# Last stage of a gated Fourier and Mish layer: unused weight buffers become operand pairs, and y is added to the first half's results by an accumulating transfer

## The chip, the cores and the metric

The kernel runs on one core of one Trainium2 chip. The metric is device time in microseconds (us), the median of three runs. Before the change it is 867.15 us (866.71 to 867.68).

## What is computed

x is 2048 tokens by 640. The reference, cut to what matters:

```
g = sigmoid((x * gate_w).sum(-1))
y = real(DFT_seq(DFT_hidden(x)))            # as products with cosine and sine matrices
h = x @ w1 + b1                             # 640 -> 1728
b = mish(h) @ w2                            # 1728 -> 640
out = g * y + (1 - g) * b
```

All in float32. The kernel holds every product transposed: features in partitions, tokens in columns, in tiles of 128 by 512. The tokens make four column tiles t = 0 to 3.

## The kernel before

**Products.** A float32 operand is split in two halves for TensorE: h is the value rounded by ScalarE's copy to the type float32r (line 316), l is the rest, which VectorE gets by a subtraction (line 317). A product is three matmuls, hh, hl and lh (`mm3`, line 326). Moving operands lie in pairs of 128x512 tiles (pool R, ten pairs, named r0h, r0l and so on), stationary ones in pairs of 128x640 tiles (pool W, 26 pairs, named w0h, w0l and so on). The large products use a two-by-two scheme with seven block products in place of eight (`Stage` for the sums of the stationary side, `Problem` for the moving side), so many operands are sums of loaded tiles, made by VectorE (`tt`, line 287, recorded as line 289).

**Stages.** First the DFT along the sequence (four problems), then the DFT along the features (two problems, `hd`), whose results, already multiplied by g, are stored as y in memory (`ysc`, 20 tiles of 128x512, names y). Then w1 and Mish, stored in memory as act (`asc`); for tiles t = 2 and 3 act is multiplied by 1 - g at once (`out_act`, line 639). Last comes the product with w2, as two problems (`ou`, line 814): the first half for t = 0 and 1, the second for t = 2 and 3. Each has three parts: `first`, `second`, `third`. Both `first` parts run ahead, and the partial sums of the second half's are stored in memory (names po) and loaded again at the head of its `second` (lines 421 to 424).

**How y gets in.** In the second half (`y` given) the y tiles are loaded and added into the sums as the work goes on, since act was scaled before (`add_y`, line 481). In the first half (`y` is None, `q` is 1 - g) each of ten results is multiplied by 1 - g after its last matmul (`done`, line 535, and `give`, line 543), and `plus` (line 548) loads the y tile into a buffer of pool FS and adds it with VectorE; then `put_out` stores the result on SyncE's queue.

**Order and buffers.** The code doesn't issue instructions as it runs. It makes a graph of operations (`Graph.add`), each with an engine and a planned duration, and `Graph.run` (line 121) plans it: an event simulation at build time with one list of ready operations per engine, sorted by the time at which each is wanted. TensorE's order is fixed, one matmul each 0.2267 us; all wants are worked back from it (`wants`, line 84). Work that empties a bank, and what follows such work of ScalarE or VectorE, is `prompt` and is wanted early. An operation takes buffers from pools when it is planned to start; buffers are kept back for whoever wants them earlier (`granted`, line 146). The planned order is then the order of each engine's instructions and of each queue, and an instruction waits, in order, for what it depends on. A transfer is planned as 2.2 us plus its bytes at 370 GB/s, all transfers one after another (`dma`, line 267). Loads are on SyncE's queue (SP, SPq in the profile, line 276), stores of intermediate results on GpSimd's (POOL, line 285), stores of the output on SyncE's.

**Pools.** FS holds 18 tiles of 128x512 (names f), X six of 128x640 (names x). When nobody asks for an x tile any more, freed x tiles pass to FS (`heir`, lines 206 to 208): a name x on a 128x512 operation of the last stage is such a tile. W has no heir. The last stage's weights take three pairs for each of six row blocks, two shared pairs (`T2`) and two for the remaining rows (`w2_rest`).

Of the kernel before, what the change touches and what calls it, by code (L numbers as in the profile page):

```python
# [12 lines left out]
OP = mybir.AluOpType  # L13

S, D, F = 2048, 640, 1728
P = 128
N = 512
# [7 lines left out]
NR, NFS, NX, NW = 10, 18, 6, 26  # L25
# [22 lines left out]
class Graph:  # L48
# [72 lines left out]
    def run(self, pools):  # L121

        self.wants()
        for op in self.ops:
            for v in op.vals:
                if v.pool and (v.ask is None or op.want < v.ask[0]):
                    v.ask = op.want, op.n, id(v)
        for op in self.ops:
            for v in op.vals:
                if v.pool and v.ask[1] == op.n:  # L130
                    also = [u.ask[0] for u in op.vals if u.pool is v.pool and u is not v]
                    if also:
                        v.ask = min(v.ask, (max(also), op.n, id(v)))
        for p in pools:
            p.asks = sorted({v.ask for op in self.ops for v in op.vals if v.pool is p})
            p.soon = sorted({v.ask for op in self.ops if op.prompt for v in op.vals if v.pool is p and v.ask[1] == op.n})
        missing = {op.n: len(op.deps) for op in self.ops}
        free = {e: 0.0 for e in ("PE", "ACT", "DVE", "SP", "POOL")}
        ready = {e: [] for e in free}
        pe = [op.n for op in self.ops if op.engine == "PE"][::-1]  # L140
        for op in self.ops:
            if not missing[op.n]:
                insort(ready[op.engine], (op.want, op.n))
        events, now, left, dma = [], 0.0, len(self.ops), 0.0

        def granted(op, blocked):
            for v in op.vals:
                if v.pool and v.t is None:
                    if v.pool in blocked:
                        return False  # L150
                    p, n = v.pool, bisect_left(v.pool.asks, v.ask)
                    if not op.prompt:
                        n += bisect_left(p.soon, (v.ask[0] + AHEAD,)) - bisect_left(p.soon, v.ask)
                    if len(p.free) <= n:
                        blocked.add(v.pool)
                        return False
            return True

        while left:
            began = False  # L160
            for e, line in ready.items():
                if free[e] > now + 1e-9 or not line:
                    continue
                if e == "PE":
                    i = next((i for i, x in enumerate(line) if x[1] == pe[-1]), None)
                    if i is not None and not granted(self.ops[pe[-1]], set()):
                        i = None
                else:
                    blocked = set()
                    i = next((i for i, x in enumerate(line) if granted(self.ops[x[1]], blocked)), None)  # L170
                if i is None:
                    continue
                op = self.ops[line.pop(i)[1]]
                if e == "PE":
                    pe.pop()
                for v in op.vals:
                    if v.pool and v.t is None:
                        v.pool.asks.remove(v.ask)
                        if v.ask in v.pool.soon:
                            v.pool.soon.remove(v.ask)  # L180
                        v.t = v.pool.free.pop(0)
                op.emit()
                free[e] = now + op.hold
                if e in ("SP", "POOL"):
                    dma = max(now + DELAY, dma) + op.moves
                    end = dma + 0.1
                else:
                    end = now + op.took + 0.03
                heapq.heappush(events, (end, op.n))
                left -= 1  # L190
                began = True
            if began:
                continue
            times = [t for e, t in free.items() if t > now + 1e-9 and ready[e]]
            if events:
                times.append(events[0][0])
            assert times, ("stuck", left, pe and self.ops[pe[-1]].at, [(p.name, len(p.free)) for p in pools])
            now = max(now, min(times))
            while events and events[0][0] <= now + 1e-9:
                op = self.ops[heapq.heappop(events)[1]]  # L200
                for v in op.vals:
                    v.left -= 1
                    if not v.left and v.pool:
                        p = v.pool
                        p.free.append(v.t)
                        if p.heir and not p.asks:
                            p.heir.free += [p.part(t) for t in p.free]
                            p.free = []
                for a in op.after:
                    missing[a.n] -= 1  # L210
                    if not missing[a.n]:
                        insort(ready[a.engine], (a.want, a.n))
# [8 lines left out]
def fnet_mish_gate(ctx: ExitStack, tc: tile.TileContext, xn, xt, c_re, c_im, wd_re, wd_im,  # L221
                   w1a, w1b, b1a, b1b, w2, gw, out):
    nc = tc.nc
# [5 lines left out]
    def pair(name, n):  # L229
        return sb.tile([P, n], F32R, name=f"{name}h"), sb.tile([P, n], F32R, name=f"{name}l")  # L230

    psum = Pool("psum", [pp.tile([P, N], F32, name=f"ps{i}") for i in range(8)])
    R = Pool("r", [pair(f"r{i}", N) for i in range(NR)])
    FS = Pool("f", [sb.tile([P, N], F32, name=f"f{i}") for i in range(NFS)])
    X = Pool("x", [sb.tile([P, D], F32, name=f"x{i}") for i in range(NX)], FS, lambda t: t[:, :N])
    W = Pool("w", [pair(f"w{i}", D) for i in range(NW)])
    b1s = Val(t=sb.tile([P, NF], F32, name="b1s"))
    gcol = Val(t=sb.tile([P, KS], F32, name="gcol"))
    qcol = Val(t=sb.tile([P, KS], F32, name="qcol"))
# [6 lines left out]
    def scratch(name, n, rows=P):  # L246
        return [[dram(f"{name}{i}_{t}", rows) for t in range(TG)] for i in range(n)]

    usc, ysc = scratch("u", 2 * KD), scratch("y", KD)
# [6 lines left out]
    def whole(*vals):  # L256
        return [(v, None) for v in vals]

    def dve(emit, r, w, n=N, more=0.0):
        took = 0.15 + n / 960 + more  # L260
        return G.add("DVE", emit, r, w, took, took - 0.083)
# [5 lines left out]
    def dma(queue, emit, r, w, size):  # L267
        op = G.add(queue, emit, r, w, DELAY + size / RATE, 0.605 if queue == "SP" else 1.0)
        op.moves = size / RATE
        return op  # L270
# [3 lines left out]
    def load(pool, src, of=None, rows=P, cols=N, queue="SP"):  # L274
        v = Val(pool)
        dma(queue, lambda: ISSUE[queue].dma_start(v.t[:rows, :cols], src() if callable(src) else src),  # L276
            whole(of) if of else [], whole(v), rows * cols * 4)
        return v

    def load_of(pool, d, rows=P):  # L280
        return load(pool, lambda: d.t, d, rows)

    def store(d, v, rows=P, queue=None):
        queue = queue or STORES
        dma(queue, lambda: ISSUE[queue].dma_start(d.t, v.t[:rows]), whole(v), whole(d), rows * N * 4)  # L285

    def tt(o, a, b, op, cut=(slice(None),) * 3, rows=slice(None), n=N):
        (x, y, z) = cut
        dve(lambda: nc.vector.tensor_tensor(o.t[rows, x], a.t[rows, y], b.t[rows, z], op=op),  # L289
            whole(a, b), whole(o), n)  # L290
# [50 lines left out]
    class Stage:  # L341
# [17 lines left out]
        def top(self, k):  # L359
            if k in self.XA:  # L360
                return
            w = self.XA[k] = Val(W)
            g = load(X, self.row(k), cols=D)
# [3 lines left out]
        def low(self, k):  # L367
# [10 lines left out]
            if k // KD not in self.T2:  # L378
                self.T2[k // KD] = Val(W)
            b, c = self.XB[k], self.XT13[k] = Val(W), Val(W)  # L380
            split(self.XA[k], 3, t, 2 * P, 2 * P)
# [10 lines left out]
    class Problem:  # L392
# [154 lines left out]

        def plus(self, f, d, t):
            if self.st is fin and not self.y:
                tt(f, f, load_of(FS, ysc[d][t]), OP.add)  # L550
            self.finish(d, t, f)

        def end(self):
# [37 lines left out]
    def w1_block(f):  # L591
        if f in W1:
            return
        ga, gb, t = load(X, w1a[f], cols=D), load(X, w1a[f + FP], cols=D), Val(X)
        a, b, c = W1[f] = Val(W), Val(W), Val(W)
        if f // KD not in T2B:
            T2B[f // KD] = Val(W)
        split(a, 0, ga, 0, D)
# [11 lines left out]
    def w1_rest():  # L610
        if W1C:
            return
        W1C.append(Val(W))
        split(W1C[0], 0, load(X, w1a[FC - 1], cols=D), 0, D)
# [185 lines left out]
    def put_u(m):  # L800
        return lambda d, t, f: store(usc[m * KD + d][t], f)
# [92 lines left out]
```

## Time and profile before

| | us |
|---|---|
| median of three runs | 867.15 |
| profiled execution, device time | 868.05 |
| its span, first to last instruction | 866.3 |
| TensorE (PE) busy | 859.0 |
| VectorE (DVE) busy | 678.2 |
| ScalarE (ACT) busy | 463.1 |
| GpSimd (POOL) busy | 69.4 |

One execution is recorded by the profiler; times in its views count from its first instruction. A row such as `DVE L289 TENSOR_TENSOR f<-f,f` names engine, line of the kernel (that of the helper which records the operation), operation, and output and inputs by tile names, in most views without buffer numbers; ps is a bank of PSUM. What stands in square brackets behind a row is the engine's idle time ahead of it and who ended it. The chain that ended last is followed back from the last instruction to what released each step.

### The profile page before, as it was taken

The numbers are of one execution on the slowest core, as the hardware profiler recorded it, in microseconds if no ns is written. First come the engines' busy times: TensorE is split into PE (matmuls) and PEld (weight loads), VectorE is DVE, ScalarE is ACT, GpSimd is POOL, SyncE is SP. The second block draws the span as 40 slices with busy tenths as digits, with TensorE's granted clock in tenths as the row PEclk, the third lists the DMA queues.
The fourth block names the chain that finished last, engine by engine and source line by source line (L and its number), as shares of the span: only waits on it lengthen the run. The fifth ranks groups of instructions, "written<-read, shape, count | busy, mean of one in ns | idle before, by whom it ended". The sixth has DMA issues, their size and how long they took to land.

```text
span 866.3 us, 11982 instructions
## 1 busy us (share of the span) xinstructions
PE 859.0 (99%) x3772; PEld 709.1 (82%) x3772; DVE 678.2 (78%) x1213; ACT 463.1 (53%) x849; POOL 69.4 (8%) x132
## 2 busy tenths in 40 slices
PE   9999999999999999999999999999999999999998
PEld 7888888888888888888888888888888888887786
DVE  7999997976785577998878999925576997739991
ACT  7765536544553444677553666735655754531541
POOL 0000002001100200002002012111111100000000
PEclk9999999999999999999999999999999999999999
DMA  9986979864956565759854959456363778626943
GB/s 317 345 283 217 361 216 385 282 217 135 362 171 203 171 255 147 258 192 320 311 183 166 341 208 359 158 197 203 126 212 127 269 273 288 188 84 209 369 169 121
DMA packets 103232, 203.50 MB, mean 235 GB/s; under 512 B 12801, under 2 KB 15233, under 8 KB 103169
## 3 DMA queue, kind: packets, MB, share of 16 engines
q1 hardware_dynamic: 92912, 169.57, 58.4%
q0 software_dynamic: 10112, 33.04, 10.3%
q8 instruction: 29, 0.48, 0.2%
q14 instruction: 35, 0.28, 0.1%
q10 hardware_dynamic: 144, 0.13, 0.0%
HBM read 164.40 MB, written 38.29 MB: 234 GB/s over the span
## 4 chain that ended last, share of the span: by engine, by line
PE 96%; DMA 2%; DVE 1%; issue 0%; ACT 0%; SPq 0%; ACTq 0%; DVEq 0%
PE ps L322 96%; DMA out_dram<-f 1%; DVE f L289 1%; DMA f<-act 1%; DMA x<-in_xn_dram 1%; DVE x L289 0%; SPq L276 0%; DVE r7l L317 0%; DVE r9l L317 0%; ACT r1h L316 0%; ACT r7h L316 0%; DVE r3l L317 0%; DVE f L563 0%; ACT f L561 0%; ACT w0h L310 0%
## 5 line engine op out<-in xcount | busy, mean ns | idle before, releaser
L289 DVE TENSOR_TENSOR f<-f,f 128x512 f32<-128x512 f32 x314 | 211.0, 686 | 15.8 <-DMA f<-in_c_im_dram 7.6
L289 DVE TENSOR_TENSOR f<-ps,f 128x512 f32<-128x512 f32 x100 | 65.3, 685 | 42.9 <-PE ps L322 42.7
L298 ACT ACTIVATE f<-ps 128x512 f32<-128x512 f32 x128 | 74.8, 594 | 37.5 <-PE ps L322 29.9
L285 POOL DMA_DIRECT2D u<-f x40 | 21.5, 540 | 321.5 <-DVE f L289 310.3
L316 ACT ACTIVATE r1h<-f 128x512 fp32r<-128x512 f32 x43 | 27.1, 630 | 32.1 <-PE ps L322 15.7
L316 ACT ACTIVATE r2h<-f 128x512 fp32r<-128x512 f32 x41 | 25.9, 631 | 31.1 <-PE ps L322 24.8
L316 ACT ACTIVATE r8h<-f 128x512 fp32r<-128x512 f32 x41 | 25.8, 630 | 28.3 <-PE ps L322 20.9
L586 ACT ACTIVATE f<-f,b1s 128x512 f32<-128x512 f32 x36 | 25.7, 723 | 28.2 <-DVE f L289 28.1
L316 ACT ACTIVATE r9h<-f 128x512 fp32r<-128x512 f32 x39 | 24.5, 629 | 28.0 <-PE ps L322 18.9
L316 ACT ACTIVATE r4h<-f 128x512 fp32r<-128x512 f32 x39 | 24.5, 629 | 27.4 <-PE ps L322 24.2
L285 POOL DMA_DIRECT2D act<-f x52 | 28.2, 542 | 134.6 <-DVE f L289 72.4
L316 ACT ACTIVATE r6h<-f 128x512 fp32r<-128x512 f32 x39 | 24.5, 628 | 25.0 <-PE ps L322 18.7
L316 ACT ACTIVATE r0h<-f 128x512 fp32r<-128x512 f32 x40 | 25.1, 627 | 23.7 <-PE ps L322 18.1
L317 DVE TENSOR_TENSOR r7l<-f,r7h 128x512 fp32r<-128x512 f32 x41 | 28.2, 688 | 12.0 <-ACT r7h L316 11.8
L316 ACT ACTIVATE r5h<-f 128x512 fp32r<-128x512 f32 x41 | 25.7, 628 | 21.9 <-PE ps L322 15.4
L317 DVE TENSOR_TENSOR r2l<-f,r2h 128x512 fp32r<-128x512 f32 x41 | 28.2, 688 | 11.7 <-ACT r2h L316 11.5
L316 ACT ACTIVATE r7h<-f 128x512 fp32r<-128x512 f32 x41 | 25.7, 628 | 21.4 <-PE ps L322 12.5
L317 DVE TENSOR_TENSOR r8l<-f,r8h 128x512 fp32r<-128x512 f32 x41 | 28.2, 688 | 10.3 <-ACT r8h L316 10.2
L317 DVE TENSOR_TENSOR r5l<-f,r5h 128x512 fp32r<-128x512 f32 x41 | 28.2, 688 | 9.8 <-ACT r5h L316 9.7
L317 DVE TENSOR_TENSOR r6l<-f,r6h 128x512 fp32r<-128x512 f32 x39 | 26.8, 688 | 11.2 <-ACT r6h L316 11.0
L317 DVE TENSOR_TENSOR r0l<-f,r0h 128x512 fp32r<-128x512 f32 x40 | 27.5, 688 | 10.2 <-ACT r0h L316 10.0
L317 DVE TENSOR_TENSOR r1l<-f,r1h 128x512 fp32r<-128x512 f32 x43 | 29.6, 688 | 7.2 <-ACT r1h L316 7.1
(1830 smaller groups left out, 2639.0 us busy)
## 6 DMA issues: line engine op xcount, KB each, us to landing
f<-in_c_re_dram SPq DMA_DIRECT2D x128, 256.0 KB, 4.9
f<-in_c_im_dram SPq DMA_DIRECT2D x128, 256.0 KB, 4.4
f<-act SPq DMA_DIRECT2D x86, 256.0 KB, 5.1
f<-u SPq DMA_DIRECT2D x80, 256.0 KB, 4.7
act<-f POOLq DMA_DIRECT2D x52, 256.0 KB, 3.0
f<-in_xt_dram SPq DMA_DIRECT2D x44, 256.0 KB, 5.2
u<-f POOLq DMA_DIRECT2D x40, 256.0 KB, 5.7
x<-in_xn_dram SPq DMA_DIRECT2D x25, 320.0 KB, 5.0
```

The lines of the kernel that those rows point to most:

```text
L285: dma(queue, lambda: ISSUE[queue].dma_start(d.t, v.t[:rows]), whole(v), whole(d), rows * N * 4)
L289: dve(lambda: nc.vector.tensor_tensor(o.t[rows, x], a.t[rows, y], b.t[rows, z], op=op), whole(a, b), whole(o), n)
L298: act(lambda: nc.scalar.activation(o.t, a.t, AF.Copy, scale=scale), whole(a), whole(o))
L316: act(lambda: nc.scalar.activation(r.t[0][:, :N], src.t[:, :N], AF.Copy), whole(src), [(r, 0)])
L317: dve(lambda: nc.vector.tensor_tensor(r.t[1][:, :N], src.t[:, :N], f32(r.t[0][:, :N]), op=OP.subtract), whole(src) + [(r, 0)], [(r, 1)])
L322: G.add("PE", lambda: nc.tensor.matmul(bank.t, w.t[wn][:, k * P:k * P + P], x.t[xn_][:, :N], start, stop, skip_group_check=True), [(w, (k, ...
L586: act(lambda: nc.scalar.activation(o.t[rows], src.t[rows], AF.Mish, **more), whole(src, table) + whole(b1s) * bias, whole(o), more=0.1)
```

## The change

W gets R as its heir: when nobody asks for a weight pair any more, free ones pass to R, cut to 512 columns. The handing on becomes a function, `bequeath`, that is called not only when a buffer is freed but also when one is taken, so that buffers that are free when the last ask is served pass on at once; this holds for X and FS as well.

In the first half of the last stage, `plus` no longer loads y into a buffer and adds it with VectorE. A transfer on GpSimd's queue reads the y tile from memory and adds it to the result tile in SBUF (`accum_op=OP.add`). It is planned as 2.8 times the bytes of a plain transfer. The store to the output, still on SyncE's queue, follows it.

```
+        def bequeath(p):
+            if p.heir and not p.asks:
+                p.heir.free += [p.part(t) for t in p.free]
+                p.free = []
...
                         v.t = v.pool.free.pop(0)
+                        bequeath(v.pool)
...
                         p.free.append(v.t)
-                        if p.heir and not p.asks:
-                            p.heir.free += [p.part(t) for t in p.free]
-                            p.free = []
+                        bequeath(p)
...
-    W = Pool("w", [pair(f"w{i}", D) for i in range(NW)])
+    W = Pool("w", [pair(f"w{i}", D) for i in range(NW)], R, lambda t: (t[0][:, :N], t[1][:, :N]))
...
+    def add_from(v, d):
+
+        dma("POOL", lambda: nc.gpsimd.dma_start(v.t, d.t, accum_op=OP.add), whole(v, d), whole(v), 2.8 * P * N * 4)
...
         def plus(self, f, d, t):
             if self.st is fin and not self.y:
-                tt(f, f, load_of(FS, ysc[d][t]), OP.add)
+                add_from(f, ysc[d][t])
             self.finish(d, t, f)
```

## The prediction

> **What bounds the kernel now.** I read the page's first part, then the chain that ended last, then TensorE's timeline where that chain leaves TensorE, and then, at that place, what the late instructions waited for. The page says that TensorE is busy nearly always:
>
> ```profile
> PE 859.0 (99%) x3772; PEld 709.1 (82%) x3772; DVE 678.2 (78%) x1213; ACT 463.1 (53%) x849; POOL 69.4 (8%) x132
> ```
>
> The chain, in order of time (start, length, what), shows where it isn't:
>
> ```profile
> 6.76 772.58 PE ps L322 x3406
> ...
> 789.57 0.70 DVE f L289
> 790.26 0.02 issue
> 790.28 0.32 SPq L276
> 790.60 0.05 issue
> 790.65 5.96 DMA out_dram<-f
> 796.61 0.02 issue
> 796.63 5.50 DMA f<-act
> ...
> 806.92 55.39 PE ps L322 x243
> 862.32 0.02 issue
> 862.34 0.39 ACT f L561
> ```
>
> For 772.58 us and for the last 55.39 us the chain is nothing but matmuls, 772.58 / 3406 = 0.2268 us apart. The count of matmuls is not touched by the change, nor is the start (6.76 us) or the tail after 862.34. So all that can be gained lies in the 28 us between the two long pieces, where the first half of the last product hands over to the second. TensorE's timeline there (start, length, ...):
>
> ```profile
> 797.07 0.39 PE L322 MATMUL ps<-r5h,w11h 128*128 128x512 f32 x1
> 797.54 0.50 PE L322 MATMUL ps<-r5l,w11h 128*128 128x512 f32 x1
> 797.88 0.40 PE L322 MATMUL ps<-r5h,w11l 128*128 128x512 f32 x1
> 798.98 0.50 PE L322 MATMUL ps<-r5h,w23h 128*128 128x512 f32 x1 [0.70 <-ACT ps L298]
> 799.32 0.39 PE L322 MATMUL ps<-r5l,w23h 128*128 128x512 f32 x1
> ...
> 805.69 0.39 PE L322 MATMUL ps<-r7h,w9l 128*128 128x512 f32 x1
> 806.03 0.50 PE L322 MATMUL ps<-r3h,w20h 128*128 128x512 f32 x1
> 806.92 0.50 PE L322 MATMUL ps<-r3l,w20h 128*128 128x512 f32 x1 [0.39 <-DVE r3l L317]
> 807.26 0.39 PE L322 MATMUL ps<-r3h,w20l 128*128 128x512 f32 x1
> ```
>
> Matmul records overlap, so the idle column (0.70 and 0.39) understates the loss; starts tell it. First stall: 799.32 - 797.07 = 2.25 us for four steps that take 4 x 0.2268 = 0.91, a loss of **1.34 us**. Second: 807.26 - 805.69 = 1.57 us for three steps (0.68), a loss of **0.89 us**. Together **2.23 us**, 0.26% of the run. That is the cap on what this change can win.
>
> Why they are late is read on ScalarE and on SyncE's queue:
>
> ```profile
> 795.61 0.60 ACT L298 ACTIVATE ps<-x 128x512 f32<-128x512 f32 x1 [14.32 <-DMA x<-po]
> ...
> 798.32 0.60 ACT L298 ACTIVATE ps<-f 128x512 f32<-128x512 f32 x1 [0.52 <-DMA f<-po]
> ```
>
> ```profile
> 777.31 0.32 SPq L276 DMA_DIRECT2D f<-y  x1
> ...
> 790.28 0.32 SPq L276 DMA_DIRECT2D x<-po  x1
> ...
> 792.17 1.26 SPq L276 DMA_DIRECT2D f<-po  x1
> ```
>
> First stall: the second half restarts from partial sums kept in memory (po). Their two loads were issued at 790.28 and 792.17, the last copy into a bank began at 798.32 and TensorE went on at 798.98. The chain says why the loads were late: the load at 790.28 had to wait until an add of VectorE (789.57, 0.70 long) had read the buffer that it was to fill. Second stall: a load of act issued at 796.63 waited for a store to release its buffer (790.65 + 5.96), landed after 5.50 us, and went through sums and splits to r3l, for which TensorE waited until 806.92. Both are one shortage: **full-width buffers (18 f and 6 heirs from x)**, of which ten go in turn to y, the first half's addends (a load of y is still issued at 777.31, ahead of the stalled ones). By stretches (length, then busy time and count of TensorE, its weight loads, VectorE, ScalarE and GpSimd, granted clock, share of the DMA engines, GB/s):
>
> ```profile
> 766.00:780.00 14.00, 14.00 (x63) 11.60 (x62) 6.57 (x11) 4.89 (x8) 0.00 (x0) 1.00 0.22 57
> 780.00:795.00 15.00, 15.00 (x68) 12.42 (x67) 15.00 (x27) 0.60 (x1) 0.00 (x0) 1.00 0.45 138
> 795.00:820.00 25.00, 23.82 (x102) 18.55 (x101) 21.91 (x37) 12.86 (x22) 0.00 (x0) 1.00 1.04 384
> ```
>
> Before the handover the DMA engines are at 0.22 of their time and VectorE at 6.57 of 14 us (buffers are full, nobody can run ahead); then VectorE is full for 15 us with results while ScalarE makes almost no operands (0.60 us); then the DMA engines are full at 384 GB/s to catch up.
>
> **The change part by part.** 1. *Ten adds leave VectorE.* The first half gives ten result tiles; each loses an add of this kind:
>
> ```profile
> L289 DVE TENSOR_TENSOR f<-f,f 128x512 f32<-128x512 f32 x8 | 5.4, 684 | 0.0
> ```
>
> ```profile
> 781.76 0.68 DVE L289 TENSOR_TENSOR f<-f,f 128x512 f32<-128x512 f32 x1
> 782.36 0.68 DVE L289 TENSOR_TENSOR f<-ps,f 128x512 f32<-128x512 f32 x1
> ```
>
> Length 0.68, but they start 0.60 apart: 10 x 0.60 = 6.0 us of VectorE, taken out of the stretch around the handover in which VectorE is full (15.00 of 15 us). Elsewhere VectorE has idle time, so the sum counts this only through the stalls: the splits that follow the results can start some 6 us sooner.
>
> 2. *Ten y loads leave SyncE's queue*, and ten buffers that y held up to the adds come free before the handover. The loads next in line (act, po, the second half's y) take them, in the stretch with DMA at 0.22. Ten transfers more there are 10 x 0.26 MB / 384 GB/s = 7 us of the engines against 0.78 x 14 = 11 us idle. That removes the cause of both stalls.
>
> 3. *Four more operand pairs.* Of 26 weight pairs the last stage uses 3 x 6 + 2 + 2 = 22 (three per block row, two shared, two for the remainder), so four pass to R when the last weight buffer is taken. With next to no new operand from 780 to 795, ten pairs lasted to the first stall at 797, 17 us or 1.7 us each; fourteen last 24 us. Before, ScalarE waited for TensorE to free a pair in the stretch before, 720 to 779 (us in total, times, longest):
>
> ```profile
> ACT r8h L316 <- PE ps L322: 5.5, 3, 2.7
> ACT r6h L316 <- PE ps L322: 5.4, 2, 4.6
> ```
>
> That slack makes the four splits ahead free; without it they would cost 4 x 0.6 us of each engine at the handover, which VectorE's 6.0 us cover. The earlier handing on of free x buffers changes at most a few loads by a few us in the same slack: nothing.
>
> 4. *Ten accumulating transfers on GpSimd's queue.* GpSimd issues nothing in any of the stretches shown (x0), so nothing is queued behind an accumulate that waits for VectorE's product. Issue cost, 0.54 us, from the y stores; the nearest rows for landing are the y loads':
>
> ```profile
> L285 POOL DMA_DIRECT2D y<-f x20: 539/539/556, 466.1 to 522.5; - x20
> ...
> DMA to landing us min/median/max: 2.3/4.6/7.8
> ```
>
> ```profile
> f<-y SPq DMA_DIRECT2D x13, 256.0 KB, 4.9
> ```
>
> No accumulate is in the trace. Its share of the DMA engines is no less than a load's 0.68 us (0.26 MB at 384 GB/s); the far end is that the ten go one after another at the median landing of a y load, 4.9 us each, 49 us in all. I take the planner's own coefficient in the diff, 2.8 loads, 1.9 us each, 19 us for the ten; it is nearer the low end, and the engines work on several transfers at once in the trace. Of these 19 us, 7 us are paid back by the loads of step 2. The rest, 12 us, falls on 780 to 820, where the engines were full, but 7 us or more of that stretch's loads are now earlier and TensorE eats only three loads per 21 matmuls (3 x 0.26 MB in 4.8 us, 165 GB/s of 384). Cost to TensorE: **0**; without the cover of operands made ahead, up to the 12 us less the idle time.
>
> The Trainium skill ("Collectives: The Full Stack", "The bandwidth ceiling: the fold count and why AG ≠ RS ≠ AR") says that an add inside a transfer needs two source reads and so runs at about half a copy's rate. By that an accumulate would be two loads, an estimate of 1.4 us each, and the sum would be the same.
>
> 5. *The store waits for the accumulate*, on SyncE's queue, in order: loads are queued behind it and TensorE, later, waits for them. In the planner the store has lost its due time (only vector and scalar work makes its follower prompt), so it goes when no load can. I cost this at 0, hidden by 24 us of pairs.
>
> **Sum.** The profiled execution took 868.05 us (span 866.3 and 1.8 around it), 0.90 over the median of 867.15. 868.05 - 1.34 - 0.89 + 0 = 865.8; against the median 867.15 - 2.23 = **864.9 us**.
>
> **The rivals.** *A. The shortage moves.* The order of all engines in the last 150 us is planned anew; one of the two stalls stays, or a new one of its size comes, since results now hold buffers longer (product, accumulate, store at lowest priority). For: six of the ten result tiles are taken fresh from the same pool, and a transfer of y takes up to 7.8 us to land. Against: a result plus its y were two tiles, now one. It would give 867.15 - 0.89 = 866.3, or up to no gain.
>
> *B. Slower: SyncE's queue stands still.* If the ten accumulates go at the far end, 49 us, where the planner reckons 19, the last lands 30 us after the time at which the planner puts its store into SyncE's queue. Every load behind stands that long. It decides from the point where the delay exceeds the pairs' 24 us: 30 - 24 = 6 us lost in place of the stalls, 864.9 + 6 = about 870. For: stores did hold loads before (5.96 us in the chain), and the engines are full. Against: several transfers overlap, and a queue that stands gives the engines to the accumulates.
>
> Its rule in the Trainium skill ("DMA: Bandwidth & Descriptors", "Issuing engines are not separate DMA queues"): transfers issued on another queue run on the same 16 DMA engines and save issue time only. The trace can't show it for accumulates; it agrees that the engines are what is short at 1.04.
>
> *C. It doesn't do what it says*: the four pairs pass on too late or the planner doesn't use them. Then the y part alone remains, which already frees more buffers than the stalled loads lacked; a result between A and the forecast.
>
> **How the numbers follow.** A measurement of this kernel can tell about 0.2%, 1.7 us, from no change; the forecast's 2.23 lies little above it. Both stalls gone: 0.58, of which 0.06 would measure as no change. A and C: 0.25. B: 0.17. So faster 0.52, within 0.2% 0.31, slower 0.17. The range goes from the cap with the spread of the runs (about 0.5 us) below it, 864.3, to B, 869.9.
>
> **What would show it.** Right: no gap between matmul starts over 0.25 us from 780 to 820; po loaded and copied before TensorE asks; ten y rows on GpSimd at 0.54 us; operands written to w3, w4, w13, w14; DMA well over 57 GB/s from 766 to 780. Wrong: SyncE waiting on f<-y before a store of out, accumulates landing over 10 us after issue, new gaps in TensorE after 800, or a tail after 862.

## The result, and the profile after

| | before | after |
|---|---|---|
| median of 20 runs, us | 867.15 (866.39 to 868.24) | 865.86 (864.72 to 866.23) |
| profiled execution, device time, us | 868.05 | 866.02 |
| its span, us | 866.3 | 864.3 |

The ratio of the times, after to before, is **0.9981, 95% interval 0.9975 to 0.9988**: faster by 1.6 us, between 1.0 and 2.2. (The two medians alone lie 1.29 us apart.) The forecast was 864.9 us, 2.23 us faster (0.9974), just outside this interval.

Line numbers are 4 to 8 higher in the kernel after (L276 is L280, L285 is L289, L289 is L297, L298 is L306, L317 is L325, L322 is L330). The chain that ended last now has one piece of matmuls where it had two with 28 us of other work between them:

```profile
6.97 853.21 PE ps L330 x3762
860.18 0.02 issue
```

853.21 / 3762 = 0.2268 us per matmul over the whole run. TensorE waits nowhere between 780 and 820; by stretches (columns as in the prediction):

```profile
766.00:780.00 14.00, 14.00 (x64) 11.59 (x63) 7.04 (x11) 5.00 (x9) 0.00 (x0) 1.00 0.22 77
780.00:795.00 15.00, 15.00 (x68) 12.43 (x67) 15.00 (x26) 5.74 (x10) 8.91 (x10) 1.00 0.80 157
795.00:820.00 25.00, 25.00 (x112) 20.72 (x111) 11.26 (x18) 5.40 (x9) 0.00 (x0) 1.00 1.07 343
```

From 795 to 820 TensorE was busy 23.82 us and is now busy 25.00. ScalarE makes 5.74 us of operands and copies in the 15 us in which it made almost none. VectorE, full as before from 780 to 795, then has only 11.26 us of work where it had 21.91. The stretch before the handover hardly changed: 0.22 of the DMA engines both times (57 and 77 GB/s).

What took the place of y's loads is seen in SyncE's issues from 745 to 780 (count, size, median us to landing), before and then after:

```profile
f<-y SPq DMA_DIRECT2D x7, 256.0 KB, 2.8
...
f<-act SPq DMA_DIRECT2D x3, 256.0 KB, 2.7
```

```profile
f<-act SPq DMA_DIRECT2D x11, 256.0 KB, 3.0
...
f<-y SPq DMA_DIRECT2D x2, 256.0 KB, 3.5
```

With the buffers named x counted in, eleven loads of y and four of act have become three of y (for the second half) and fourteen of act. Most of them go out before 766.

SyncE's queue and ScalarE show the partial sums (po) of the first stall. All three loads now go out before 756; in the kernel before, two of the three went out at 790 and 792. The copies into the banks end at 787.1:

```profile
745.86 0.54 SPq L280 DMA_DIRECT2D f<-po  x1
...
753.28 0.32 SPq L280 DMA_DIRECT2D f<-po  x1
755.09 0.32 SPq L280 DMA_DIRECT2D x<-po  x1
```

```profile
785.50 0.58 ACT L306 ACTIVATE ps<-x 128x512 f32<-128x512 f32 x1
786.02 0.58 ACT L306 ACTIVATE ps<-f 128x512 f32<-128x512 f32 x1
786.54 0.58 ACT L306 ACTIVATE ps<-x 128x512 f32<-128x512 f32 x1
```

The passed-on pairs are used. The rows of tile w3h from 690 on show it written as an operand in place of a weight (w4h, w13h and w14h have such rows too):

```profile
L324 ACT ACTIVATE w3h<-f x4: 614/634/635, 709.6 to 825.0; 128x512 fp32r<-128x512 f32 x4
```

The ten accumulates (L293) in the rows of tile y (shortest, median and longest in ns), and the packets of the two queues from 780 to 820 (count, MB, share of 16 engines):

```profile
L289 POOL DMA_DIRECT2D y<-f x20: 542/542/556, 466.2 to 523.6; - x20
...
L293 POOL DMA_DIRECT2D f<-y x7: 861/1100/1573, 782.9 to 791.0; - x7
L293 POOL DMA_DIRECT2D x<-y x3: 1030/1362/1923, 787.4 to 789.2; - x3
...
DMA to landing us min/median/max: 2.3/5.7/12.7
```

```profile
q1 hardware_dynamic: 4556, 8.30, 58.8%
q0 software_dynamic: 1440, 2.62, 37.6%
```

An accumulate takes 0.376 x 40 / 10 = 1.5 us of all 16 engines; a plain 0.26 MB takes 0.588 x 40 x 0.262 / 8.30 = 0.74. Stores wait for accumulates on SyncE's queue, 5.8 us at the longest, and TensorE doesn't feel it (times waited in all, how often, longest):

```profile
SPq L289 <- DMA f<-y: 7.8, 3, 5.8
```

### The profile page after: what moved, and what is told of

It is laid out like the page before. It is cut to its first block, busy times and chain, and to the rows that moved or that the text cites. A ratio compares the mean times of both kernels' runs of the same rounds, so it can differ in the third digit from the quotient of the medians.

```text
span 864.3 us, 11968 instructions
## 1 busy us (share of the span) xinstructions
PE 857.2 (99%) x3772; PEld 709.0 (82%) x3772; DVE 672.5 (78%) x1203; ACT 463.5 (54%) x849; POOL 78.7 (9%) x142
## 4 chain that ended last, share of the span: by engine, by line
PE 99%; DMA 1%; SPq 0%; ACT 0%; DVE 0%; issue 0%; ACTq 0%
PE ps L330 99%; DMA x<-in_xn_dram 1%; SPq L280 0%; DVE x L571 0%; ACT x L569 0%; ACT w0h L318 0%; ACTq L569 0%
## 5 line engine op out<-in xcount | busy, mean ns | idle before, releaser
L297 DVE TENSOR_TENSOR f<-f,f 128x512 f32<-128x512 f32 x308 | 206.8, 686 | 17.6 <-DMA f<-in_c_im_dram 6.8
L297 DVE TENSOR_TENSOR f<-ps,f 128x512 f32<-128x512 f32 x99 | 64.8, 684 | 46.1 <-PE ps L330 39.7
L306 ACT ACTIVATE f<-ps 128x512 f32<-128x512 f32 x132 | 77.4, 595 | 37.9 <-PE ps L330 29.9
L289 POOL DMA_DIRECT2D u<-f x40 | 21.6, 543 | 321.6 <-DVE f L297 311.1
L289 POOL DMA_DIRECT2D act<-f x52 | 28.3, 545 | 132.8 <-DVE f L297 71.2
L324 ACT ACTIVATE r2h<-f 128x512 fp32r<-128x512 f32 x38 | 23.9, 630 | 27.2 <-PE ps L330 22.2
L324 ACT ACTIVATE r1h<-f 128x512 fp32r<-128x512 f32 x38 | 23.9, 629 | 24.7 <-PE ps L330 15.5
L324 ACT ACTIVATE r3h<-f 128x512 fp32r<-128x512 f32 x39 | 24.6, 629 | 21.0 <-PE ps L330 14.8
L325 DVE TENSOR_TENSOR r2l<-f,r2h 128x512 fp32r<-128x512 f32 x38 | 26.1, 688 | 10.9 <-ACT r2h L324 10.8
L325 DVE TENSOR_TENSOR r0l<-f,r0h 128x512 fp32r<-128x512 f32 x38 | 26.2, 689 | 10.3 <-ACT r0h L324 10.1
L325 DVE TENSOR_TENSOR r3l<-f,r3h 128x512 fp32r<-128x512 f32 x39 | 26.8, 687 | 9.1 <-ACT r3h L324 9.0
L325 DVE TENSOR_TENSOR r9l<-f,r9h 128x512 fp32r<-128x512 f32 x38 | 26.1, 688 | 9.5 <-ACT r9h L324 9.1
L325 DVE TENSOR_TENSOR r5l<-f,r5h 128x512 fp32r<-128x512 f32 x38 | 26.1, 688 | 9.4 <-ACT r5h L324 9.3
L325 DVE TENSOR_TENSOR r8l<-f,r8h 128x512 fp32r<-128x512 f32 x39 | 26.8, 688 | 8.3 <-ACT r8h L324 8.2
L325 DVE TENSOR_TENSOR r4l<-f,r4h 128x512 fp32r<-128x512 f32 x39 | 26.8, 687 | 7.9 <-ACT r4h L324 7.7
```

The costliest lines, as they stand in the source:

```text
L306: act(lambda: nc.scalar.activation(o.t, a.t, AF.Copy, scale=scale), whole(a), whole(o))
L324: act(lambda: nc.scalar.activation(r.t[0][:, :N], src.t[:, :N], AF.Copy), whole(src), [(r, 0)])
L325: dve(lambda: nc.vector.tensor_tensor(r.t[1][:, :N], src.t[:, :N], f32(r.t[0][:, :N]), op=OP.subtract), whole(src) + [(r, 0)], [(r, 1)])
```

## The experiments

The theory is that both stalls of TensorE came from a shortage of full-width buffers, of which y held ten. The rivals are the four pairs, VectorE's ten adds, and, for the other side, SyncE's queue standing behind accumulates. The last two columns are worked out from all matmul starts of one profile: what the steps between them take over 0.2268 us, summed over a stretch.

| kernel | ratio to before, 95% interval | lost 780 to 812, us | lost 812 to 845, us |
|---|---|---|---|
| before, first profile | | 2.3 | 0 |
| before_again | 1.0003 (0.9995 to 1.0012) | 1.5 | 0 |
| the change | 0.9981 (0.9975 to 0.9988) | 0 | 0 |
| adds_no_loads | 0.9982 (0.9973 to 0.9991) | 0 | 0 |
| loads_no_adds | 0.9993 (0.9984 to 1.0001) | 0.9 | 0 |
| pairs_alone | 1.0000 (0.9992 to 1.0009) | 1.6 | 0 |
| y_alone | 1.0003 (0.9994 to 1.0012) | 0 | 1.7 |
| y_alone_due | 1.0000 (0.9991 to 1.0009) | 0 | 1.7 |
| y_alone_pool | 1.0004 (0.9996 to 1.0013) | 0 | 2.3 |
| y_alone_narrow | 1.0001 (0.9993 to 1.0010) | 0 | 1.7 |
| due | 0.9981 (0.9972 to 0.9989) | 0 | 0 |
| planned_one | 1.0006 (0.9998 to 1.0014) | 0 | 2.2 |
| planned_five | 1.0051 (1.0039 to 1.0063) | 0 | 5.5 |
| added_twice | 1.0055 (1.0043 to 1.0068) | 0 | 6.6 |

**before_again**: the kernel before, no edit.

> The kernel before, unchanged, timed against itself. Every theory expects a ratio of 1.000 within about 0.001. Its second profile shows whether the two stalls of TensorE (1.34 us near 797, 0.89 us near 806 in the first profile) are of a fixed size: if they are, the forecast of 2.23 us stands and the measured 1.3 to 1.7 us has lost something elsewhere; if the second profile has less than 2 us of them, the first was a large sample and the forecast was mis-sized by it.

TensorE's timeline at the same two places:

```profile
796.98 0.39 PE L322 MATMUL ps<-r5h,w11h 128*128 128x512 f32 x1
...
798.45 0.50 PE L322 MATMUL ps<-r5h,w23h 128*128 128x512 f32 x1 [0.29 <-ACT ps L298]
798.78 0.39 PE L322 MATMUL ps<-r5l,w23h 128*128 128x512 f32 x1
...
805.39 0.40 PE L322 MATMUL ps<-r3h,w20h 128*128 128x512 f32 x1
806.08 0.50 PE L322 MATMUL ps<-r3l,w20h 128*128 128x512 f32 x1 [0.29 <-DVE r3l L317]
806.42 0.39 PE L322 MATMUL ps<-r3h,w20l 128*128 128x512 f32 x1
```

The same matmuls wait for the same things, for less: (798.78 - 796.98) - 4 x 0.2268 = 0.89 and (806.42 - 805.39) - 2 x 0.2268 = 0.58, together 1.47 us where the first profile has 2.23. The places are fixed by the plan, the sizes are not.

**adds_no_loads** and **loads_no_adds**: the kernel before with one half of `plus` each.

```
-                tt(f, f, load_of(FS, ysc[d][t]), OP.add)
+                tt(f, f, f, OP.add)
```

> The kernel before, but the ten adds add each result to itself, so no y is loaded for the first half; g y is left out of the first half's output. VectorE has all its work, ten pairs as before, no accumulates; only the ten loads and their buffers are gone. Theory (full-width buffers): both stalls gone, ratio 0.998. Rival (VectorE is full for 15 us at the handover and makes no operands): the second stall stays, 0.9 us, ratio 0.999 to 1.000.

```
-                tt(f, f, load_of(FS, ysc[d][t]), OP.add)
+                tt(f, f, load_of(FS, ysc[d][t]), OP.add, (slice(0, 8),) * 3, n=8)
```

> The kernel before, but each of the ten adds covers 8 of 512 columns; so y is loaded and held as before, while VectorE loses some 0.5 us of each add (the other columns of the first half's output lack g y). The counterpart of the run that had the adds without the loads. Theory (full-width buffers): the partial sums are still loaded late, so the first stall stays, shorter by what VectorE frees sooner, ratio 0.999 to 1.000. Rival (VectorE's adds): both stalls gone, 0.998.

Without the loads both stalls are gone, with ten pairs, no accumulate, and VectorE as full as it can be (third busy time of each row):

```profile
780.00:795.00 15.00, 15.00 (x68) 12.43 (x67) 15.00 (x26) 4.62 (x8) 0.00 (x0) 1.00 0.45 155
795.00:812.00 17.00, 17.00 (x77) 14.08 (x76) 17.00 (x29) 7.67 (x13) 0.00 (x0) 1.00 1.05 367
```

So VectorE being full doesn't by itself make the stalls; leaving out y's loads and their buffers removes them. This run also leaves out the loads' work for the DMA engines.

Without the adds' work, but with the buffers held, 0.9 us are lost, and the time can't be told from no change. The po loads are as late as before (790.8 and 792.8), yet of the first stall only 0.2 us is left, and 0.7 of the second. The expectation had it the other way round: so VectorE's work has a share in how long the first stall lasts. Against this run y_alone, below, also does without the adds and moves the same y with more work of the DMA engines (1.5 us each), but without buffers for it, and has neither stall. So the buffers, not that work, make the difference. No run gives the kernel more buffers, which would be the direct test.

**pairs_alone**: the change, with the old `plus`.

```
-                add_from(f, ysc[d][t])
+                tt(f, f, load_of(FS, ysc[d][t]), OP.add)
```

> The change without the accumulating transfer: four more operand pairs, y loaded and added by VectorE as before. Theory (full-width buffers): operands move out of f buffers into four more pairs, which frees four f buffers of the ten that y holds, so part of the gain: ratio 0.999, one stall stays. Rival (pairs): the whole gain, 0.998. Rival (VectorE's ten adds): no gain, 1.000.

Nothing is gained; 1.6 us are lost as before. The theory's 0.999 was wrong, and this run alone would fit the rival of VectorE's ten adds, which adds_no_loads excludes. SyncE's queue shows that the po loads are as late as they were (790.28 and 792.17):

```profile
790.40 0.32 SPq L280 DMA_DIRECT2D f<-po  x1
...
792.29 0.90 SPq L280 DMA_DIRECT2D x<-po  x1
```

**y_alone**: the change without the heir.

```
-    W = Pool("w", [pair(f"w{i}", D) for i in range(NW)], R, lambda t: (t[0][:, :N], t[1][:, :N]))
+    W = Pool("w", [pair(f"w{i}", D) for i in range(NW)])
```

> The change without the heir of W: y is added by the accumulating transfer, ten operand pairs as before. Theory (full-width buffers were short): both stalls gone or nearly so, ratio 0.998. Rival (the four pairs matter): the ten pairs run out near 797 as before, a stall of 0.5 us or more stays, ratio 0.999 to 1.000.

Neither expectation held. Both stalls at the handover are gone, as the theory has it, yet the time is that of before: new stalls stand 20 us later. TensorE's timeline:

```profile
824.07 0.40 PE L330 MATMUL ps<-r3h,w21h 128*128 128x512 f32 x1
825.23 0.50 PE L330 MATMUL ps<-r3l,w21h 128*128 128x512 f32 x1 [0.77 <-DVE r3l L325]
```

It is not a free pair that lacks. The pair r3 stands empty for over 13 us, from its last matmul to the copy that fills it again, and r1 does so from 807 to 818:

```profile
809.47 0.39 PE L330 MATMUL ps<-r3h,w22l 128*128 128x512 f32 x1
```

```profile
823.15 0.62 ACT L324 ACTIVATE r3h<-f 128x512 fp32r<-128x512 f32 x1
```

So neither part alone brings anything, and the two together bring all of it. (Both parts keep the earlier handing on of free buffers, which no run takes alone.) Three edits of y_alone ask what makes the new stall. **y_alone_due**, in `plus`:

```
                 add_from(f, ysc[d][t])
+                self.finish(d, t, f)
+                G.ops[-1].by = G.pe + 12.0
+                return
             self.finish(d, t, f)
```

> The accumulating transfer without the four pairs, but the ten stores of the first half's results get a due time in the planner, 12 us after the last matmul planned at that place, instead of none. Theory (buffers: results wait for the low-priority store and hold f buffers too long): the stalls near 824 to 833 that the run without the four pairs showed (about 1.5 us) go, ratio 0.998. Rival (the accumulates themselves, their landing of 5 to 13 us and their double share of the DMA engines, hold the buffers): the stalls stay or move, ratio 1.000.

**y_alone_pool**, in `plus`:

```
                 add_from(f, ysc[d][t])
+                return self.finish(d, t, f, "POOL")
             self.finish(d, t, f)
```

> The accumulating transfer without the four pairs, the ten stores issued on GpSimd's queue behind their accumulates instead of SyncE's. SyncE's queue then never stands behind an accumulate (8 us in all, 5.6 at the longest, in the run without the four pairs). Rival B in small (the standing queue makes the stalls near 824): stalls gone, ratio 0.998. Theory (buffers): each result still holds its buffer as long, the next accumulate even waits behind a store, so the stalls stay, ratio 1.000 or more.

**y_alone_narrow**, in `add_from`:

```
-        dma("POOL", lambda: nc.gpsimd.dma_start(v.t, d.t, accum_op=OP.add), whole(v, d), whole(v), 2.8 * P * N * 4)
+        dma("POOL", lambda: nc.gpsimd.dma_start(v.t[:, :8], d.t[:, :8], accum_op=OP.add), whole(v, d), whole(v), 2.8 * P * N * 4)
```

> The accumulating transfer without the four pairs, planned in the same order, but each accumulate moves 8 of 512 columns (the rest of the first half's output lacks g y). Waits and order as in the run without the four pairs; only the transfers' work for the DMA engines is gone. If the accumulates' work (1.5 us of all 16 engines each, by the packets' times) makes the stalls near 824, they go: ratio 0.998. If it is the added step in the chain product, accumulate, store, or the planned order, the stalls stay: 1.000.

None of the three wins the time back. y_alone_due doesn't test what it was meant to: with the due time the ten stores leave SyncE's queue from 786.3 to 811.9, without it from 786.5 to 810.9. But in y_alone_pool the last store leaves 6 us sooner, at 805.1, and none of them stands in SyncE's queue, and 2.3 us are lost. So neither late stores nor SyncE's queue standing behind accumulates make the stalls. Nor does the accumulates' work: in y_alone_narrow the transfers of GpSimd's queue from 780 to 820 take 5.6% of the engines in place of 36.8% in y_alone, and the same two matmuls (823.67 and 824.82) stall as long.

```profile
q0 software_dynamic: 1440, 0.04, 5.6%
```

The narrow kernel has the same instructions in the same order on TensorE, VectorE, ScalarE and SyncE as y_alone. What is left is that order, and what follows from it. VectorE's timeline of y_alone:

```profile
815.34 0.69 DVE L297 TENSOR_TENSOR x<-ps,x 128x512 f32<-128x512 f32 x1 [5.02 <-PE ps L330]
815.95 0.68 DVE L325 TENSOR_TENSOR r9l<-f,r9h 128x512 fp32r<-128x512 f32 x1
```

VectorE idles 5.0 us (8.3 in the narrow kernel) because the plan put the emptying of a bank ahead of the split r9l, for which r9h was ready at 810.5. From 819 VectorE has hardly a pause left and is late at 824. The chain then goes on through a load of act that waited until ScalarE had read the buffer to be filled, so buffers are waited for here again:

```profile
820.37 0.61 ACT ps L306
...
821.37 3.70 DMA x<-act
...
827.63 34.51 PE ps L330 x150
```

The change's VectorE idles there too, 6.3 us up to 815.06. But the operands that it has split by 809 carry TensorE to 823.5; in y_alone those at hand end at 821.7, and r9 among them is half made. With ten pairs the planner made the worse order. Whether that comes from the pairs themselves, from the price of 2.8 loads that it reckons with, or from something else in the plan is not shown; no run gives the kernel with ten pairs another price.

**due**, **planned_one**, **planned_five**, **added_twice**: the whole change, with the due time of y_alone_due; with 1.0 and with 5.0 in place of 2.8; and with each accumulate made twice.

```
-        dma("POOL", lambda: nc.gpsimd.dma_start(v.t, d.t, accum_op=OP.add), whole(v, d), whole(v), 2.8 * P * N * 4)
+        dma("POOL", lambda: nc.gpsimd.dma_start(v.t, d.t, accum_op=OP.add), whole(v, d), whole(v), 1.0 * P * N * 4)
```

```
                 add_from(f, ysc[d][t])
+                add_from(f, ysc[d][t])
```

> The change as it is, with the due time for the ten stores (12 us after the last matmul planned at that place). No stall is left at the handover in the change's profile, so theory and rivals expect no difference from the change: 0.998. A slower time would mean that early stores make SyncE's queue stand.

> The change as it is, but the planner is told that an accumulate moves the bytes of one load (1.0 in place of 2.8). Stores and loads are then put into SyncE's queue for accumulates that land earlier than they do. Rival B (the queue stands behind a store): stands of over 10 us and a stall of 1 us or more, ratio 0.999 to 1.003. Theory (fourteen pairs cover it): no stall, 0.998.

> The change as it is, but the planner is told 5.0 loads in place of 2.8, 35 us of engines for the ten accumulates. The plan then holds loads back behind transfers that are in fact done. Theory: the planner believes the loads of the second half late and results held long; stalls come back only if that wait exceeds the pairs' 24 us; ratio 0.998 to 1.000. If the coefficient does not matter, 0.998 here and with 1.0.

> The change as it is, with every accumulate made twice, one after the other, so that 2 g y is added to the first half's output instead of g y. Twenty accumulates, planned at 39 us of the DMA engines. Theory (fourteen pairs are a cover of 24 us, of which the change uses a part): the results hold their buffers some 10 us longer, which uses the cover up; stalls of up to 2 us come back after 815, ratio 0.998 to 1.001. If the ratio stays at 0.998 with no gap in TensorE, the cover has more than 10 us left.

The due time changes nothing in the time. It does make SyncE's queue stand: in **due** one store waits 11.4 us for its accumulate, and TensorE loses nothing (waits of the queue from 780 to 850):

```profile
SPq L289 <- DMA f<-y: 13.2, 4, 11.4
```

The coefficient changes much, both ways. Told 1.0, the plan puts a store into SyncE's queue 10.6 us before its accumulate has landed (same stretch), and TensorE loses 2.03 us at one place:

```profile
SPq L289 <- DMA f<-y: 12.7, 3, 10.6
```

```profile
821.99 0.39 PE L330 MATMUL ps<-r4h,w8l 128*128 128x512 f32 x1
824.25 0.50 PE L330 MATMUL ps<-r4h,w8h 128*128 128x512 f32 x1 [1.87 <-ACT ps L306]
```

These are the signs that rival B named, but the stand is not shown to be the cause, since the longer one of **due** costs nothing. The chain runs from the stall back through a load of act, issued at 816.06 and landed 6.2 us later, and doesn't touch a store:

```profile
816.06 6.21 DMA x<-act
```

What in this plan makes that load late is open. Told 5.0, TensorE loses 5.5 us from 821 on, and the kernel is 0.5% slower than before, against an expected 0.998 to 1.000; the longest stand is 6.0 us there, and the cause wasn't followed further. Done twice, the accumulates cost 6.6 us of TensorE where up to 2 were expected. The chain shows results that hold their buffers longer, as the theory says: an accumulate lands after 14.24 us, its store after 12.62 more, and only then goes the load of act that the late operand is made from:

```profile
792.91 14.24 DMA f<-y
807.17 12.62 DMA out_dram<-f
819.86 7.72 DMA f<-act
```

The rest is TensorE's clock. Its timeline:

```profile
825.98 0.39 PE L330 MATMUL ps<-r5h,w21l 128*128 128x512 f32 x1
829.08 0.80 PE L330 MATMUL ps<-w13h,w11h 128*128 128x512 f32 x1 [2.71 <-ACT w13h L324]
...
830.82 0.63 PE L330 MATMUL ps<-w13h,w11h 128*128 128x512 f32 x1
831.25 0.63 PE L330 MATMUL ps<-w13l,w11h 128*128 128x512 f32 x1
...
835.35 0.39 PE L330 MATMUL ps<-w3h,w2l 128*128 128x512 f32 x1
```

0.60 us go at 823.54 (1.06 for two steps) and 2.87 at 825.98. Then the fourteen steps from 829.08 to 835.35 take 6.27 us in place of 3.18, most of them 0.43 us: TensorE's granted clock is halved after the gap (0.50 in the row below).

```profile
829.00:835.00 6.00, 5.92 (x13) 4.42 (x14) 5.25 (x9) 2.70 (x6) 0.00 (x0) 0.50 1.06 381
```

## Why the prediction was right, point by point

*What bounds the kernel, and the cap.* Right. All that was won lay in the two stalls; TensorE now runs without a gap to the end; the start (6.76 and 6.97 us) and the tail hardly moved.

*The cause.* Right in the main: full-width buffers. adds_no_loads brings the whole gain by leaving out y's loads and buffers, with VectorE as full as before. VectorE's adds had a share in the length of the first stall, though (0.2 us left in loads_no_adds, with the po loads as late), where I had called both stalls one shortage of buffers.

*The size, 1.34 + 0.89.* This term was mis-sized: it was taken from one execution, in which the stalls were large. The second profile of the same kernel has 1.47; the mean of the two is 1.85, and the measured gain is 1.6 us (1.0 to 2.2). So the time came out 0.9 us above the forecast.

*Part 1, VectorE's adds.* Priced rightly through the stalls only. loads_no_adds shortens them (0.9 against 1.5 to 2.3 us lost), with no gain that can be told.

*Part 2, the loads that take y's place.* Right in what they are, wrong in where. Loads of act and po do go out in place of y's, fourteen and three against four and one from 745 to 780. But I let them fill the stretch from 766 to 780, and its share of the DMA engines stayed at 0.22; they go mostly before 766, when the kernel before loaded y.

*Part 3, the four pairs, and rival C.* Here a step failed. I wrote that the y part alone "already frees more buffers than the stalled loads lacked; a result between A and the forecast". y_alone measured 1.0003. The old stalls went, and stalls of the same size came at 824, which is rival A. I priced the pairs only as a cover for late accumulates and a standing queue, 24 us long. y_alone_narrow and y_alone_pool take these two away and the stalls stay, so that is not what the pairs do; they change the whole plan, and how is open. That the forecast held in spite of this is in part luck: the change has both parts, and the sum had no term for what y alone would lose.

*Part 4, the accumulates.* The price of 1.9 us of the engines was high; it is 1.5, 2.0 times a load. That agrees with the Trainium skill's two source reads ("Collectives: The Full Stack", "The bandwidth ceiling: the fold count and why AG ≠ RS ≠ AR"). The issue of 0.54 us was too low, 0.86 to 1.9 on GpSimd. They land up to 12.7 us after issue, and SyncE's queue waits on them ahead of stores, both of which I had listed as signs of being wrong; TensorE felt neither.

*Part 5 and rival B, SyncE's queue.* The cost of 0 was right. The queue stands 5.8 us at the longest in the change, and 11.4 in **due**, which loses nothing either. Stands of 10.6 (planned_one, 2.2 us lost) and 11.4 us with opposite outcomes show that a stand of this length doesn't decide. No run comes near the 24 us from which I let it decide.

## What to carry to other kernels

When an engine is busy 99%, add up its late starts before anything else: they cap the gain, and what each late start waited for names the place to look. Take that sum from several profiles, since a stall's place is the plan's but its length varies between executions (2.23 and 1.47 us here). In a kernel whose order is planned ahead, a change of one operation changes all orders behind it: try its parts apart and together, and vary the price that the planner is told (1.0, 2.8 and 5.0 gave 1.0006, 0.9981 and 1.0051). And before a wait is called the cause of a loss, look for a run that has the same wait without the loss, as **due** has here.

## What the runs showed of the hardware

- An accumulating transfer of 0.26 MB from memory into SBUF takes 1.5 us of all 16 DMA engines, a plain one 0.74. GpSimd spends 0.86 to 1.9 us on its issue, where a plain store takes 0.54, and the width doesn't set this: in y_alone_narrow, with 8 of 512 columns, the row of seven of them still reads as below.

```profile
L293 POOL DMA_DIRECT2D f<-y x7: 858/1052/1541, 782.4 to 788.3; - x7
```

- After a gap of 3.10 us between matmul starts (2.71 us idle, added_twice) TensorE's granted clock was 0.50 for the next 6 us, which doubled the stall's price. In planned_five it was 0.51 from 827.40 to 830.00 after four gaps of 0.81 to 1.50 us between starts within 5.5 us. A single gap of 2.26 us in planned_one's profiled execution left the steps behind it at full speed. So the length of one gap doesn't settle it here. The Trainium skill ("TensorE: Matmul & The Clock Gate", "What's actually happening") has the clock fall after an idle window of about 3.4 us; here it fell after less.
